# Two convolution layers: the product's halves interleaved, the second chunk's transform moved onto TensorE, the first chunk's sums opened with the stream

## The chip, the core and the metric

The kernel runs on one core of one Trainium2 chip. A core has five engines that run their own instruction streams and meet only at semaphores: TensorE (PE in the profile; its weight loads are PEld), VectorE (DVE), ScalarE (ACT), GpSimd (POOL) and SyncE (SP, which here only issues transfers). TensorE writes to PSUM; VectorE and ScalarE read PSUM and SBUF. Transfers (DMA) are issued by SP, ACT or POOL and carried out by 16 DMA engines that all issuers share.

The metric is the device time of one execution in microseconds (us); lower is better.

## The reference

A stream `x` of 2048 rows by 640 channels goes through four layers, each a normalisation, a layer function and a residual sum:

```python
x = A_u
x = x + _A_ref(_layernorm(x, axis=-1), ...)   # long convolution
x = x + _B_ref(_layernorm(x, axis=-1), ...)   # attention, 32 heads of 20, one shared key and value head
x = x + _A_ref(_layernorm(x, axis=-1), ...)
x = x + _B_ref(_layernorm(x, axis=-1), ...)
```

The convolution builds one kernel of length 2048 for each channel from 128 complex exponentials, and convolves each channel of the normalised stream with it:

```python
P = jnp.exp(logdA[:, :, None] * l[None, None, :])
K = jnp.einsum("dn,dnl,dn->dl", Cc, P, dB).real
Kf = rfft(pad(K)); Uf = rfft(pad(u transposed))
y = irfft(Uf * Kf)[:L] transposed + u * Dskip
```

So a convolution layer is, per channel: transform, complex product with the kernel's spectrum, inverse transform, residual sum.

## The kernel before

**Stages.** First the kernels `K` are generated (0 to about 300 us). Then follow convolution layer a with the kernels' spectra in front of it (to about 618 us), attention layer b (to about 1693 us), convolution layer c (to about 1940 us) and attention layer d. The change lies in `conv_layer`, which makes layers a and c; only a is called with `first=True`.

**Chunks.** A layer treats the 640 channels in five chunks of 128 (`NCH` = 5), numbered c = 0 to 4. Sequence position is split over 128 partitions and 16 columns `tau`, so the stream is `x[128, 16, 640]`. A chunk passes these steps:

1. `prepare(c)`: ScalarE writes the normalised chunk into `xn` (one buffer for all chunks, so chunk c+1's values wait for chunk c's matmuls), in 128x128 pieces (L761). TensorE multiplies with the transform weights `wf`, ScalarE copies the four sums (`z0` to `z3`) from PSUM into the chunk's spectrum `A`. There are two forms. `raw` (L574 matmuls, L576 copies) takes 16 normalised pieces and transforms each of the eight residues by itself; VectorE must then begin with `halve` (L587), one sum and one difference over 2048 columns each. `dense` (L608, L610) takes 24 pieces, eight of them the negatives of others, and streams pairs of them, so that the sums and differences come out of TensorE: twice the moving columns per matmul, and no `halve`. Chunks 0 and 1 use `raw`, the others `dense`.
2. Forward `fft8`: sixteen VectorE instructions between `A` and the scratch `B` (L114, L117).
3. The complex product with the kernel's spectrum `kh`. For chunks 0 to 3 this is `spread`: VectorE computes the four real products in place, in two halves of the rows h = 0 and 1, four instructions each (L845, L846, L847, L849), and the sums and differences are left to the DMA engines: POOL issues a transfer that adds `r` onto `ar` (L848) and one that adds `ki` onto `ai` (L850), 512 KB each, four in a chunk. Chunk 4 does the whole product on VectorE (L779).
4. Inverse `whole(A, +1)`: `halve` and `fft8` again, on the sums that the transfers have left in `A`.
5. `inverse(c, g)`, g = 0 to 3: TensorE multiplies with `wi` (L804) into one PSUM bank of 512 columns per g; two banks take turns. For chunk 3 alone (`NCH - 2`) the sum is opened with a matmul of the identity and the stream's own piece (L797).
6. `residual(c, g)`: VectorE adds the bank onto the stream (L815). For chunk 3, where the bank already holds the whole sum, ScalarE copies it (L813). `turn(g)` is one residual and, for g < 2, the next `inverse` of the same chunk.

**Order.** The layer runs under a manual schedule: each of PE, ACT and DVE executes in the order the program states, and stalls on the first instruction whose inputs are late. Around chunk c the program states: `spread(c)`; the load of the next `kh` on SP (it waits for `spread(c)`'s transfers, since there is one `kh` buffer, L711); the forward transform of chunk c+1 with the four turns of chunk c-1 woven in at places 2, 6, 10 and 14; `prepare(c+2)`; `whole(A)` of chunk c; `inverse(c, 0)` and `inverse(c, 1)`. So TensorE's order is: transform 0, transform 1, transform 2, inverse 0, transform 3, inverse 1, transform 4, inverse 2, inverse 3, inverse 4. During chunk 3 ScalarE also takes sums for the next normalisation, and the next attention layer's weights are made (layer a) or loaded (layer c, L926).

Of the kernel before, what the change touches and what calls it, by code (L numbers as in the profile page):

```python
# [16 lines left out]
ALU = mybir.AluOpType  # L17
# [9 lines left out]
NCH = D // DC  # L27
# [76 lines left out]
def fft8(nc, A, B, sg, low=None):  # L104

    ADD, SUB = ALU.add, ALU.subtract
    plus, minus = (ADD, SUB) if sg < 0 else (SUB, ADD)  # L110
    calls = []

    def tt(*a):
        calls.append(lambda: nc.vector.tensor_tensor(*a))  # L114

    def stt(*a):
        calls.append(lambda: nc.vector.scalar_tensor_tensor(*a, op0=ALU.mult, op1=ADD))  # L117

    low = A if low is None else low
    tt(B[:, 0:4], low[:, 0:4], low[:, 4:8], ADD)  # L120
    tt(B[:, 4:8], low[:, 0:4], low[:, 4:8], SUB)
    tt(B[:, 8:12:3], A[:, 8:10], A[:, 13:11:-1], plus)
    tt(B[:, 10:8:-1], A[:, 8:10], A[:, 13:11:-1], minus)
    tt(A[:, 0:2], B[:, 0:2], B[:, 2:4], ADD)
    tt(A[:, 8:10], B[:, 0:2], B[:, 2:4], SUB)
    tt(B[:, 0:2], A[:, 10:15:4], A[:, 11:16:4], ADD)
    if sg < 0:
        tt(B[:, 2:4], A[:, 11:16:4], A[:, 10:15:4], SUB)
    else:
        tt(B[:, 2:4], A[:, 10:15:4], A[:, 11:16:4], SUB)  # L130
    tt(A[:, 4:14:9], B[:, 4:6], B[:, 7:5:-1], plus)
    tt(A[:, 12:4:-7], B[:, 4:6], B[:, 7:5:-1], minus)
    if sg < 0:
        tt(B[:, 12:16:3], B[:, 0:3:2], B[:, 3:0:-2], ADD)
        tt(B[:, 14:12:-1], B[:, 0:3:2], B[:, 3:0:-2], SUB)
    else:
        tt(B[:, 12:16:3], B[:, 2::-2], B[:, 1:4:2], SUB)
        tt(B[:, 14:12:-1], B[:, 2::-2], B[:, 1:4:2], ADD)
    sp, sm = (RT_HALF, -RT_HALF) if sg < 0 else (-RT_HALF, RT_HALF)
    f0, f2, f1, f3s = B[:, 8:10], B[:, 10:12], B[:, 12:14], B[:, 15:13:-1]  # L140
    stt(A[:, 2:4], f1, RT_HALF, f0)
    stt(A[:, 10:12], f1, -RT_HALF, f0)
    stt(A[:, 6:16:9], f3s, sp, f2)
    stt(A[:, 14:6:-7], f3s, sm, f2)
    return calls


def weave(calls, between):

    for i in range(len(calls) + 1):  # L150
        for n, call in between:
            if n == i or (i == len(calls) and n > i):
                call()
        if i < len(calls):
            calls[i]()


class Net:
# [579 lines left out]
    def conv_layer(self, nm, first):  # L738
# [3 lines left out]
        tc, nc, cv = self.tc, self.nc, self.cvp  # L742
        B = self.B
        tt = nc.vector.tensor_tensor
        with tc.manual_schedule(engines={mybir.EngineType.PE, mybir.EngineType.Activation,
# [14 lines left out]
            def normal(out, c, tau, r, b):  # L760
                nc.scalar.activation(out, X(c, tau), AF.Identity, scale=r[:, tau : tau + 1],  # L761
                                     bias=b[:, tau : tau + 1])

            def normals(xn, c, t):

                for j in range(2):
                    i = 4 * j + t
                    normal(xn[:, i], c, 8 * j + t, rs, nmr)
                    normal(xn[:, 8 + 2 * i], c, 8 * j + t + 4, rs, nmr)
                    normal(xn[:, 9 + 2 * i], c, 8 * j + t + 4, rsm, nmrm)  # L770

            def new_xn(c):
                return cv.tile([P, 24, DC], F32, tag="xn", bufs=1, name=f"xn{nm}{c}")

            def m(a, c_):
                return a.rearrange("p (s c) d -> p s c d", c=2)[:, :, c_]
# [12 lines left out]
            def stream(c, g):  # L789
                return self.x[:, FIRST[g] : 16 : 4, c * DC : (c + 1) * DC]  # L790

            def inverse(c, g, A):
                y = self.ps1(f"y{nm}{c}{g}")
                v = A.rearrange("p s (k d) -> p s k d", k=2)
                whole = c == NCH - 2
                if whole:
                    nc.tensor.matmul(y, self.ident, stream(c, g), start=True, stop=False)  # L797
                for s in range(4):
                    tau = TAUS[4 * g + s]
                    t, j = tau % 8, tau // 8  # L800
                    i = 0
                    for kk in range(2):
                        for c_ in range(2):
                            nc.tensor.matmul(y[:, s * DC : (s + 1) * DC], self.wi[:, t, j, c_, kk],  # L804
                                             v[:, 2 * t + c_, kk], start=(i == 0 and not whole),
                                             stop=(i == 3 and (s == 3 or not whole)))
                            i += 1
                return y

            def residual(c, g, y):  # L810
                y = y.rearrange("p (t d) -> p t d", t=4)
                if c == NCH - 2:
                    nc.scalar.activation(stream(c, g), y, AF.Copy)  # L813
                else:
                    tt(stream(c, g), y, stream(c, g), ALU.add)  # L815
                if c == NCH - 1:
                    self.stats_last(g)


            def prepare(c):  # L820

                xn = new_xn(c)
                for t in range(4):
                    if c < 2:
                        for tau in (t + 4, t + 12, t, t + 8):
                            normal(xn[:, tau], c, tau, rs, nmr)
                    else:
                        normals(xn, c, t)
                return (self.raw if c < 2 else self.dense)(xn, f"{nm}{c}", (c + 1) % 3)

            As = {0: prepare(0)}
            khs = {0: self.load_spectrum(0)}
            self.wi = cv.tile([P, 8, 2, 2, 2, P], F32, tag="wi", name="wi")
# [4 lines left out]
            def spread(A, kh):  # L838


                add = nc.gpsimd.dma_start
                for h in range(2):
                    s = slice(4 * h, 4 * h + 4)
                    ar, ai, kr, ki, r = m(A, 0)[:, s], m(A, 1)[:, s], m(kh, 0)[:, s], m(kh, 1)[:, s], R[:, s]
                    nc.vector.scalar_tensor_tensor(r, ai, -1.0, ki, op0=ALU.mult, op1=ALU.mult)  # L845
                    tt(ki, ar, ki, ALU.mult)  # L846
                    tt(ar, ar, kr, ALU.mult)  # L847
                    add(ar, r, accum_op=ALU.add)  # L848
                    tt(ai, ai, kr, ALU.mult)  # L849
                    add(ai, ki, accum_op=ALU.add)  # L850

            turn = None
            for c in range(NCH):
                A = As.pop(c)
                if c == NCH - 1:
                    late = [(1, lambda turn=turn: turn(0)), (2, lambda turn=turn: turn(1)),
                            (4, lambda turn=turn: turn(2)), (5, lambda turn=turn: turn(3))]
                    late = sorted(late + [(3 + k, a[0]) for k, a in enumerate(pieces)]
                                  + [(5 + k, a[1]) for k, a in enumerate(pieces)], key=lambda a: a[0])
                    weave(product(A, khs.pop(c)) + fft8(nc, A, B, +1), late)  # L860
                else:
                    spread(A, khs.pop(c))
                    khs[c + 1] = self.load_spectrum(c + 1)
                    woven = [] if turn is None else [
                        (n, lambda turn=turn, g=g: turn(g)) for g, n in enumerate((2, 6, 10, 14))]
                    N = As[c + 1]
                    weave(self.whole(N, -1) if c == 0 else fft8(nc, N, B, -1), woven)
                    if c + 2 < NCH:
                        As[c + 2] = prepare(c + 2)
                    if c + 2 == NCH - 1:  # L870
                        self.wfs.pop().close()
                    if c == NCH - 2:
                        scr = new_xn("s").rearrange("p a d -> p (a d)")

                        def dump(n):
                            return scr[:, 1280 + NA * (n % 4) : 1280 + NA * (n % 4) + NA]

                        self.stats_setup(nm)
                        for g in range(4):
                            self.stats_first(g, dump)  # L880
                        pieces = self.attn_weights(scr, nm == "a")
                    weave(self.whole(A, +1), ())
                ys = [inverse(c, g, A) for g in range(2)]

                def turn(g, c=c, A=A, ys=ys):

                    residual(c, g, ys[g])
                    if g < 2:
                        ys.append(inverse(c, g + 2, A))
# [489 lines left out]
```

## Time and profile before

| what | value |
|---|---|
| three runs | 3024.99, 3022.26, 3023.30 us |
| median | 3023.3 us |
| the profiled execution | 3024.13 us |
| its span, first to last instruction | 3022.3 us |
| TensorE, VectorE, ScalarE busy in the span | 92%, 46%, 80% |
| mean granted TensorE clock | 0.951 |

A line of the timeline reads: start, duration, engine, source line, operation, destination and sources, shapes, count of merged instructions, and in brackets how long the engine had been idle before and which instruction ended that wait. `Aa`, `za`, `ya`, `xna` are the spectrum, the forward sums, the inverse sums and the normalised chunk of layer a; `Ac`, `zc`, `yc`, `xnc` those of layer c. An fp32 matmul shows as two records, so an `inverse` of 16 matmuls is 32 records, and a chunk's inverse 128. A row of the view by stretches reads: stretch, its length, then busy time and count for PE, PEld, DVE, ACT and POOL, the granted TensorE clock, the mean busy share of the 16 DMA engines, and GB/s. "DMA to landing" is the time from the start of the issue to the last byte.

### The profile page before, as it was taken

Reading aid. Unit: us, or ns where it says so; the run is one execution under the profiler, and the core shown is the slowest. Engines: PE = TensorE matmul, PEld = TensorE weight load, DVE = VectorE, ACT = ScalarE, POOL = GpSimd, SP = SyncE. Lnnn points to the kernel's source line nnn. Section 1 sums busy time; section 2 is a strip of 40 time slices with the busy share of each in tenths; the row PEclk is TensorE's granted clock in tenths of the full one; section 3 lists DMA queues with packets and bytes.
Section 4 is the critical chain, followed back from the end, with each engine's and each line's share of the span. In section 5 each row is a group of like instructions: output and inputs, shape, how many; then the busy total and the mean of one; then the engine's idle time right before and its main releaser. Section 6 shows DMA issues by size and latency. Waiting matters only on the chain. (4 is left out here: it accounts for less than half of the span.)

```text
span 3022.3 us, 52462 instructions
## 1 busy us (share of the span) xinstructions
PE 2769.4 (92%) x21696; PEld 1266.8 (42%) x21696; DVE 1384.6 (46%) x1784; ACT 2421.5 (80%) x2894; POOL 86.3 (3%) x149
## 2 busy tenths in 40 slices
PE   2676978898999999999999888798999999999999
PEld 0333978775233323333233678673233233333233
DVE  7999899942122232322323499721222223222223
ACT  5888351444999999999999524238999999999997
POOL 0001001000000000000000011000000000000000
PEclk9656999999999999999999989899999999999999
DMA  6114555433200010100000256131100100110100
GB/s 145 33 22 112 175 154 112 97 116 115 81 22 25 22 27 21 27 24 23 25 22 20 86 112 145 39 130 56 28 24 23 43 22 25 39 28 21 43 19 23
DMA packets 126000, 175.60 MB, mean 58 GB/s; under 512 B 59460, under 2 KB 81988, under 8 KB 122132
## 3 DMA queue, kind: packets, MB, share of 16 engines
q1 hardware_dynamic: 102680, 137.70, 15.7%
q0 software_dynamic: 21104, 33.45, 5.5%
q8 instruction: 175, 2.87, 0.4%
q10 hardware_dynamic: 1968, 0.98, 0.1%
q14 instruction: 73, 0.60, 0.1%
HBM read 95.22 MB, written 48.04 MB: 47 GB/s over the span
## 5 line engine op out<-in xcount | busy, mean ns | idle before, releaser
L1177 ACT ACTIVATE pt<-scd 128x1024 f32<-128x1024 f32 x1024 | 942.2, 1116 | 6.9 <-PE scd L1173 5.5
L1177 ACT ACTIVATE pt<-scb 128x1024 f32<-128x1024 f32 x1024 | 942.1, 1116 | 6.5 <-PE scb L1173 5.1
L1187 PE MATMUL pod<-pt,vt 128*32 128x512 f32 x4096 | 546.9, 606 | 4.4 <-DVE on L1204 0.2
L1187 PE MATMUL pob<-pt,vt 128*32 128x512 f32 x4096 | 546.4, 605 | 4.4
L1173 PE MATMUL scb<-qpb,kt 62*128 62x512 f32 x2048 | 385.8, 451 | 5.9 <-DVEq L1122 5.6
L1173 PE MATMUL scd<-qpd,kt 62*128 62x512 f32 x2048 | 385.7, 451 | 5.9 <-PEq L1122 5.5
L1173 PEld LDWEIGHTS scd<-qpd,kt 62*128 62x128 f32 x2048 | 166.1, 185 | 402.2 <-ACT pt L1177 392.4
L1173 PEld LDWEIGHTS scb<-qpb,kt 62*128 62x128 f32 x2048 | 166.1, 185 | 401.6 <-ACT pt L1177 391.9
L1235 DVE TENSOR_TENSOR x<-pyd,x 128x320 f32<-128x320 f32 x146 | 71.8, 492 | 560.7 <-PE pyd L1247 560.7
L1235 DVE TENSOR_TENSOR x<-pyb,x 128x320 f32<-128x320 f32 x146 | 71.8, 492 | 547.5 <-PE pyb L1247 547.5
L1207 DVE RECIPROCAL rc<-rc 128x512 f32<-128x512 f32 x62 | 207.9, 3353 | 2.1
L1187 PEld LDWEIGHTS pod<-pt,vt 128*32 128x32 f32 x4096 | 80.6, 108 | 177.4 <-issue 159.5
L1187 PEld LDWEIGHTS pob<-pt,vt 128*32 128x32 f32 x4096 | 80.6, 108 | 177.5 <-issue 159.5
L804 PE MATMUL yc<-Ac,wi 128*128 128x128 f32 x640 | 80.2, 291 | 32.1 <-DVE Ac L114 20.4
L804 PE MATMUL ya<-Aa,wi 128*128 128x128 f32 x640 | 79.8, 290 | 32.2 <-DVE Aa L114 22.8
L1247 PE MATMUL pyb<-wo,ot 128*32 128x320 f32 x1168 | 105.3, 432 | 0.0
L1247 PE MATMUL pyd<-wo,ot 128*32 128x320 f32 x1168 | 105.3, 432 | 0.0
L804 PEld LDWEIGHTS yc<-Ac,wi 128*128 128x128 f32 x640 | 79.7, 207 | 34.9 <-DVE x L815 11.8
L804 PEld LDWEIGHTS ya<-Aa,wi 128*128 128x128 f32 x640 | 79.1, 206 | 35.1 <-DVE Aa L114 24.0
L610 ACT ACTIVATE Aa<-za 128x1024 f32<-128x1024 f32 x12 | 12.3, 1025 | 101.6 <-PE za L608 101.6
L608 PE MATMUL zc<-xnc,wf 128*128 128x256 f32 x384 | 85.3, 384 | 2.4 <-ACT xnc L761 2.3
L608 PE MATMUL za<-xna,wf 128*128 128x256 f32 x384 | 83.7, 380 | 2.7 <-ACT xna L761 2.7
(323 smaller groups left out, 3110.3 us busy)
## 6 DMA issues: line engine op xcount, KB each, us to landing
Akh<-kh SPq DMA_DIRECT2D x10, 2048.0 KB
kh<-Ak SPq DMA_DIRECT2D x5, 2048.0 KB
qhd<-qh SPq DMA_DIRECT2D x40, 256.0 KB
qld<-ql SPq DMA_DIRECT2D x40, 256.0 KB
qpb<-qhd SPq DMA_DIRECT2D x256, 40.0 KB
qpd<-qhd SPq DMA_DIRECT2D x256, 40.0 KB
ot<-on SPq DMA_DIRECT2D x216, 40.0 KB
wf<-in_c_wf POOLq DMA_DIRECT2D x16, 512.0 KB, 8.0
```

The costliest lines, as they stand in the source:

```text
L608: nc.tensor.matmul(zv[:, :, c, kk], self.wf[:, t + 4 * h, j, c, kk], x, start=(n == 0), stop=(n == 3))
L610: nc.scalar.activation(A.rearrange("p (o s) d -> p o s d", o=2)[:, :, 2 * t : 2 * t + 2], z.rearrange("p (c o e) -> p o c e", c=2, o=2), A ...
L804: nc.tensor.matmul(y[:, s * DC : (s + 1) * DC], self.wi[:, t, j, c_, kk], v[:, 2 * t + c_, kk], start=(i == 0 and not whole), stop=(i == 3 ...
L1173: nc.tensor.matmul(sc[:, 512 * par : 512 * par + 512], kt[rows, 128 * t : 128 * t + 128], qps[nb, hg, pr][rows], start=True, stop=True)
L1177: nc.scalar.activation(pt, sc, AF.Exp, scale=SCALE)
L1187: nc.tensor.matmul(po[32 * j : 32 * j + 32], vt[:, t], pts[step, j // 2][:, 512 * (j % 2) : 512 * (j % 2) + 512], start=(t == 0), stop=(t ...
L1207: nc.vector.reciprocal(rc, rc)
L1235: nc.vector.tensor_tensor(xh, py, xh, ALU.add)
L1247: nc.tensor.matmul(py[j : j + m], o[:, 128 * i + j : 128 * i + j + m], w[:, 320 * half : 320 * half + 320], start=start, stop=stop)
```

## The change

Three edits, all in `conv_layer`:

- The residual of chunk 0 is treated like that of chunk 3: the sum in PSUM is opened with identity times stream, and ScalarE copies it back instead of VectorE adding. Both layers.
- `halved` is the number of chunks that use `raw`. It is 2 in layer c, as before, and 1 in layer a: there chunk 1 uses `dense`, and its forward transform is `fft8` without `halve`.
- `spread` issues its four steps for both halves in turn (step 1 for h = 0 and 1, step 2 for both, and so on), where it did all four for h = 0 and then for h = 1. The transfers stay behind the instruction that makes their target. Chunks 0 to 3 of both layers.

```diff
@@ inverse / residual
-                whole = c == NCH - 2
+                whole = c in (0, NCH - 2)
...
-                if c == NCH - 2:
+                if c in (0, NCH - 2):
                     nc.scalar.activation(stream(c, g), y, AF.Copy)
                 else:
                     tt(stream(c, g), y, stream(c, g), ALU.add)
@@ prepare
+            halved = 1 if first else 2
+
...
-                    if c < 2:
+                    if c < halved:
                         for tau in (t + 4, t + 12, t, t + 8):
                             normal(xn[:, tau], c, tau, rs, nmr)
                     else:
                         normals(xn, c, t)
-                return (self.raw if c < 2 else self.dense)(xn, f"{nm}{c}", (c + 1) % 3)
+                return (self.raw if c < halved else self.dense)(xn, f"{nm}{c}", (c + 1) % 3)
@@ spread
+                ops = [[], [], [], []]
                 for h in range(2):
...
-                    nc.vector.scalar_tensor_tensor(r, ai, -1.0, ki, op0=ALU.mult, op1=ALU.mult)
-                    tt(ki, ar, ki, ALU.mult)
-                    tt(ar, ar, kr, ALU.mult)
-                    add(ar, r, accum_op=ALU.add)
-                    tt(ai, ai, kr, ALU.mult)
-                    add(ai, ki, accum_op=ALU.add)
+
+                    def fourth(ai=ai, kr=kr, ki=ki):
+                        tt(ai, ai, kr, ALU.mult)
+                        add(ai, ki, accum_op=ALU.add)
+
+                    def third(ar=ar, kr=kr, r=r):
+                        tt(ar, ar, kr, ALU.mult)
+                        add(ar, r, accum_op=ALU.add)
+
+                    ops[0].append(lambda r=r, ai=ai, ki=ki: nc.vector.scalar_tensor_tensor(
+                        r, ai, -1.0, ki, op0=ALU.mult, op1=ALU.mult))
+                    ops[1].append(lambda ar=ar, ki=ki: tt(ki, ar, ki, ALU.mult))
+                    ops[2].append(third)
+                    ops[3].append(fourth)
+                for a in ops:
+                    for call in a:
+                        call()
@@ the loop over chunks
-                    weave(self.whole(N, -1) if c == 0 else fft8(nc, N, B, -1), woven)
+                    weave(self.whole(N, -1) if c + 1 < halved else fft8(nc, N, B, -1), woven)
```

## Prediction, made before the changed kernel was run

> **What bounds the kernel now.** I read the view by stretches first, since the span's shares mix stages: the two attention layers fill most of it and the change does not touch them, so they can only move in time.
>
> ```profile
> span 3022.3 us, 52462 instructions
> ```
>
> ```profile
> 389.30:476.30 87.00, 61.57 (x385) 57.10 (x386) 85.79 (x107) 32.67 (x73) 10.31 (x8) 0.86 0.55 124
> 476.30:560.30 84.00, 84.00 (x515) 77.39 (x514) 77.24 (x92) 27.23 (x67) 10.61 (x9) 1.00 0.54 111
> 1795.60:1880.00 84.40, 84.40 (x516) 77.40 (x514) 77.62 (x93) 27.61 (x69) 10.26 (x8) 1.00 0.53 116
> ```
>
> From chunk 1's transform to the end of chunk 0's inverse (389 to 476 us in layer a) VectorE works 85.8 of 87 us and TensorE 61.6. From there to the last forward transform TensorE works all 84 us at full clock and VectorE waits. Layer c has the same second half. So VectorE sets when TensorE's unbroken run begins, and TensorE sets its length: work taken off VectorE pays only if TensorE can start its run earlier. The timeline of TensorE (layer a, then c) shows where it waits:
>
> ```profile
> 407.95 27.46 PE L608 MATMUL za<-xna,wf 128*128 128x256 f32 x126 [0.46 <-ACT xna L761]
> 448.24 9.95 PE L804 MATMUL ya<-Aa,wi 128*128 128x128 f32 x64 [12.83 <-DVE Aa L114]
> 467.56 8.87 PE L804 MATMUL ya<-Aa,wi 128*128 128x128 f32 x64 [9.37 <-DVE x L815]
> 476.27 27.79 PE L608 MATMUL za<-xna,wf 128*128 128x256 f32 x128
> 577.32 1.02 PE L797 MATMUL ya<-x,ident 128*128 128x512 f32 x2
> 581.75 1.02 PE L797 MATMUL ya<-x,ident 128*128 128x512 f32 x2
> ```
>
> ```profile
> 1766.42 7.31 PE L804 MATMUL yc<-Ac,wi 128*128 128x128 f32 x64
> 1785.38 10.36 PE L804 MATMUL yc<-Ac,wi 128*128 128x128 f32 x64 [11.66 <-DVE x L815]
> 1795.58 27.79 PE L608 MATMUL zc<-xnc,wf 128*128 128x256 f32 x128
> ```
>
> Waits of 12.83, 9.37 and 11.66 us stand in chunk 0's inverse. Two of them end with a residual (L815): TensorE needs the PSUM bank back and VectorE reaches the addition only after the next product. The waits cost twice: 64 records that take 7.31 us without a break take 9.95 and 10.36 after one (the mean clock of that stretch is 0.86).
>
> **Edit 1, chunk 0's residual on ScalarE (both layers).** Removed: four VectorE additions at 0.60 each (466.82 to 467.42 below) and the wait for them. Added: an identity matmul per g. The period from one opened sum to the next is 581.75 - 577.32 = 4.43 us, so an opened inverse takes 17.7. Moved: four copies enter ScalarE's queue ahead of the 24 pieces of chunk 3, which before were written long in advance.
>
> ```profile
> 389.28 6.26 ACT L761 ACTIVATE xna<-x,nmra,rsa 128x128 f32<-128x128 f32 x16
> 405.49 0.87 ACT L761 ACTIVATE xna<-x,nmra,rsa 128x128 f32<-128x128 f32 x2
> 436.37 0.87 ACT L761 ACTIVATE xna<-x,nmra,rsa 128x128 f32<-128x128 f32 x2
> 581.95 0.60 ACT L813 ACTIVATE x<-ya 128x512 f32<-128x512 f32 x1 [3.83 <-PE ya L804]
> ```
>
> The last copy can start 0.20 us after the sums (581.95 against 581.75), takes 0.60, overlaps its successor by 0.1, and only then come chunk 3's pieces: 0.7. From the first piece to the end of a dense transform is 407.95 + 27.46 - 405.49 = 29.92 us. Chunk 3's transform thus ends 30.6 us after chunk 0's inverse, where 27.79 would do: 2.8 us of new wait, in each layer, not hidden by anything.
>
> **Edit 2, chunk 1 dense in layer a.** VectorE loses `halve`, 428.18 - 423.65 = 4.53 us. TensorE gains twice the columns. Its pieces start at 389.28 as before; the transform ends at 389.28 + 29.92 = 419.20. Chunk 2's pieces follow 0.96 later (436.37 against 435.41), and its transform ends at 420.16 + 29.92 = 450.08, 14.7 later than now. The cover is the 12.83 and 9.37 us of waiting.
>
> **Edit 3, the product's order.** The VectorE rows:
>
> ```profile
> 414.06 1.23 DVE L845 SCALAR_TENSOR_TENSOR Ra<-Aa,Akh 128x1024 f32<-128x1024 f32 x1
> 415.32 1.23 DVE L846 TENSOR_TENSOR Akh<-Aa,Akh 128x1024 f32<-128x1024 f32 x1
> 416.58 1.22 DVE L847 TENSOR_TENSOR Aa<-Aa,Akh 128x1024 f32<-128x1024 f32 x1
> 417.72 1.22 DVE L849 TENSOR_TENSOR Aa<-Aa,Akh 128x1024 f32<-128x1024 f32 x1
> ...
> 423.65 2.29 DVE L587 TENSOR_TENSOR B<-Aa 128x2048 f32<-128x2048 f32 x1
> ...
> 428.18 2.35 DVE L114 TENSOR_TENSOR B<-B 128x1024 f32<-128x1024 f32 x2
> ...
> 439.37 2.29 DVE L587 TENSOR_TENSOR B<-Aa 128x2048 f32<-128x2048 f32 x1
> ...
> 454.97 1.22 DVE L845 SCALAR_TENSOR_TENSOR Ra<-Aa,Akh 128x1024 f32<-128x1024 f32 x1
> ...
> 466.82 0.69 DVE L815 TENSOR_TENSOR x<-ya,x 128x512 f32<-128x512 f32 x1
> 467.42 1.28 DVE L114 TENSOR_TENSOR B<-Aa 128x512 f32<-128x512 f32 x2
> ...
> 1772.80 1.22 DVE L845 SCALAR_TENSOR_TENSOR Rc<-Ac,Akh 128x1024 f32<-128x1024 f32 x1
> ...
> 1824.47 2.36 DVE L114 TENSOR_TENSOR B<-Ac 128x1024 f32<-128x1024 f32 x2 [1.49 <-ACT Ac L610]
> ...
> 1866.39 2.36 DVE L114 TENSOR_TENSOR B<-Ac 128x1024 f32<-128x1024 f32 x2 [1.49 <-ACT Ac L610]
> ...
> 1881.55 2.29 DVE L587 TENSOR_TENSOR B<-Ac 128x2048 f32<-128x2048 f32 x1
> ```
>
> L845 and L846 are followed 1.26 us after their start by an instruction that overwrites what they read; L847 by an independent one after 1.14. Interleaved, all eight are spaced 1.14: 9.1 instead of 9.6 us, 0.47 saved per product. [...]
>
> The other side is the transfers. The first add now stands behind the fifth product instead of the third.
>
> ```profile
> 418.39 1.33 POOL L848 DMA_DIRECT2D Aa<-Ra  x1 [94.01 <-DVE Aa L847]
> ...
> 424.03 1.41 POOL L850 DMA_DIRECT2D Aa<-Akh  x1
> ...
> 1859.50 1.29 POOL L848 DMA_DIRECT2D Ac<-Rc  x1 [34.80 <-ACT Ac L610]
> ...
> 1865.37 1.26 POOL L850 DMA_DIRECT2D Ac<-Akh  x1
> ```
>
> ```profile
> DMA to landing us min/median/max: 8.6/9.2/9.8
> ```
>
> ```profile
> 420.50:432.50 12.00, 12.00 (x58) 10.55 (x57) 11.90 (x11) 2.05 (x2) 3.07 (x3) 1.00 1.18 167
> ```
>
> ```profile
> DMA to landing us min/median/max: 15.2/15.2/15.2
> ```
>
> ```profile
> 1865.33 0.32 SPq L926 DMA_DIRECT2D wh<-whd  x1
> ```
>
> The fourth add of chunk 0 lands at 424.03 + 9.8 = 433.8, 15.4 after the first issue, and meanwhile the DMA engines are busy throughout (share 1.18): the four drain one behind the other, so the last lands 15.4 after the first is issued, however close the other three follow. The first is issued 1.81 after L847 starts (418.39 - 416.58); L847 now starts 4 x 1.14 = 4.6 after the product's start, so the issue comes at 6.4 and the last landing at 21.8, where it was 19.8. The inverse transform waits for it, and behind it VectorE's whole queue; so does the next `kh` load on SP, 2 us later but with more than 10 us to spare. In chunk 3 of layer c the load L926 (SP, issued when the last transform ends) shares the engines: there the last lands 1865.37 + 15.2 - 1859.50 = 21.1 after the first issue. The load now comes earlier relative to the adds, but the same bytes drain, so I keep 21.1.
>
> [...]
>
> **The sum, layer a.** Forward 11.19 us is 428.18 to 439.37, inverse transform 15.6 is 439.37 to 454.97. VectorE: product 414.06 to 423.2; forward of chunk 1 to 434.4; last landing 435.9, so inverse transform 435.9 to 451.5. Chunk 0's first sums could start 8.9 after its start (448.24 - 439.37), at 444.8; TensorE comes at 450.08 and is the later one. Its inverse ends at 467.8, chunk 3's transform at 498.4, now 476.27 + 27.79 = 504.06: **5.6 us earlier**. VectorE then stands ready at 498.0 (inverse of chunk 1 from 473.3, landing-bound, to 488.9, product to 498.0) and needs the transform's last copy at 499.5, so TensorE stays the bound and the rest of the layer follows shifted.
>
> **The sum, layer c.** Only edits 1 and 3 act. Chunk 0's inverse runs 1766.42 to 1784.1, chunk 3's transform ends at 1814.8, now 1823.37: 8.6 earlier, ready for VectorE at 1815.9. VectorE: chunk 1's product starts at 1772.3, landing 1794.1 (the forward transform is done at 1792.6: 1.5 us of waiting), inverse to 1809.7, product to 1818.9. Now VectorE is later by 3 us. With 11.2 + 4 x 0.60 = 13.6 for the forward of chunk 3 and its turns: 1832.5 (landing 1831.5), inverse to 1848.1, product to 1857.2. The bank it returns at 1821.9 lets the last transform end 8.3 earlier than now, so VectorE's next forward starts at 1858.1 instead of 1866.39. Its inverse would start 15.16 later (1866.39 to 1881.55), at 1873.2, but the adds, first issued at 1848.1 + 6.4 = 1854.5, land 21.1 later: 1875.6. Against 1881.55 that is **5.9 us earlier**, and VectorE is busy from there to the end of the layer.
>
> Together 11.6 us. The sum is made against the profiled execution, 3024.13 us (span 3022.3 and 1.8 around it), giving 3012.5; the median of the runs is 0.8 lower, so I forecast 3011.7.
>
> **The rivals.**
> - *The adds do not bind.* If a landing counted from the last issue, no VectorE wait would arise; layer c gains 8.6, the total is 14.2, the time 3009.1. Against it: the share of 1.18 during all four. Chance 0.12.
> - *Layer a gains nothing.* Its 5.6 is a small difference: 22.2 us of waits and 4.4 of slow clock removed, against 14.7 of dense transform, 3.3 of identity matmuls and 2.8 of new wait. If the clock lagged or the pieces came later, it is eaten: 3023.3 - 5.9 = 3017.4. Against it: in 389 to 435 us the records already run at the full rate of the unbroken run (27.46 for 126). Chance 0.14.
> - *Slower: four adds in a bunch drain worse.* Now they come in pairs 4.5 us apart. They take about 3.1 us each once flowing; at 4.2 the later landings in chunks 1 to 3 eat both layers' gains, and at 4.5 each they cost 4 us in layer a and 4.8 in c: 3032. For it: chunk 3's landing of 15.2 us shows what competition does. Against it: the third and fourth already queue behind others at the same rate. Chance 0.08.
>
> **The numbers.** My case has 0.62, with its own range 3009.5 to 3015; 0.04 is left for what I have not seen. The range over the first three cases, widened a little, is 3008 to 3018. A change of 0.2% (6 us) is about what a measurement of this kernel can tell from none. My case, the first rival and half of the second lie beyond it: faster 0.83; same 0.09; slower 0.08.
>
> **What would show it.** In layer a a dense transform of chunk 1 ending near 419 and no wait of 9 us or more on TensorE until 550; chunk 0's inverse in one piece of about 17.7; some 2 us of waiting on xn before chunk 3's transform in both layers; product instructions spaced 1.14; in layer c a wait of about 1.5 us on VectorE at the inverse transform of chunk 1 and about 2.4 at chunk 3. The forecast is wrong if chunk 0's inverse still waits for VectorE, if the landings come more than 24 us after a product's start, or if the attention layers change length.

## The result, and the profile after

The changed kernel takes 3016.49 us (median of 12 runs, 3014.54 to 3019.28) against 3024.01 for the kernel before (12 runs): 7.5 us less, ratio 0.9975, 95% interval 0.9968 to 0.9983. The profiled execution took 3015.11 us. Its page and its view by stretches:

```profile
span 3013.3 us, 52501 instructions
```

```profile
389.30:476.30 87.00, 79.47 (x408) 68.46 (x409) 81.80 (x106) 35.21 (x76) 10.36 (x8) 0.98 0.54 121
472.11:556.11 84.00, 83.54 (x507) 76.58 (x507) 74.98 (x91) 34.30 (x86) 10.66 (x9) 1.00 0.56 113
1784.00:1868.00 84.00, 83.55 (x495) 76.24 (x495) 78.40 (x97) 32.72 (x81) 10.34 (x8) 0.98 0.59 126
```

In the first stretch TensorE now works 79.5 of 87 us, where it worked 61.6. Its timeline, the forward transforms of layer a, chunk 0's inverse between them, and two transforms of layer c:

```profile
391.37 0.70 PE L608 MATMUL za<-xna,wf 128*128 128x256 f32 x2 [2.26 <-ACT xna L761]
392.53 29.15 PE L608 MATMUL za<-xna,wf 128*128 128x256 f32 x126 [0.46 <-ACT xna L761]
...
425.09 27.46 PE L608 MATMUL za<-xna,wf 128*128 128x256 f32 x126 [0.46 <-ACT xna L761]
452.39 1.02 PE L797 MATMUL ya<-x,ident 128*128 128x512 f32 x2
...
465.68 1.02 PE L797 MATMUL ya<-x,ident 128*128 128x512 f32 x2
...
472.11 0.70 PE L608 MATMUL za<-xna,wf 128*128 128x256 f32 x2 [1.84 <-ACT xna L761]
473.27 27.46 PE L608 MATMUL za<-xna,wf 128*128 128x256 f32 x126 [0.46 <-ACT xna L761]
...
1734.14 29.81 PE L608 MATMUL zc<-xnc,wf 128*128 128x256 f32 x128 [2.26 <-ACT xnc L761]
...
1784.66 29.15 PE L608 MATMUL zc<-xnc,wf 128*128 128x256 f32 x126 [0.46 <-ACT xnc L761]
```

The long waits in chunk 0's inverse are gone; its sums follow each other every 4.43 us. But the 126 records of chunk 1's transform take 29.15 us and those of chunk 2's 27.46: the same instructions. The clock (the third number from the end) in the 6 us in which the slow one begins:

```profile
392.00:394.00 2.00, 1.54 (x5) 1.26 (x5) 1.97 (x4) 2.00 (x7) 0.00 (x0) 0.72 0.72 279
394.00:396.00 2.00, 2.00 (x6) 1.56 (x5) 2.00 (x4) 2.00 (x7) 0.00 (x0) 0.50 1.01 434
396.00:398.00 2.00, 2.00 (x10) 1.70 (x10) 1.97 (x4) 2.00 (x6) 0.00 (x0) 0.92 0.50 213
```

After a wait of 2.26 us TensorE was granted 0.50 of its clock from 394 to 396 us, and 0.72 and 0.92 in the 2 us on either side. VectorE's and POOL's rows show the new order of the product and the waits for the adds:

```profile
415.34 2.36 DVE L857 SCALAR_TENSOR_TENSOR Ra<-Aa,Akh 128x1024 f32<-128x1024 f32 x2
...
424.43 3.56 DVE L114 TENSOR_TENSOR B<-Aa 128x1024 f32<-128x1024 f32 x4
...
437.23 2.29 DVE L587 TENSOR_TENSOR B<-Aa 128x2048 f32<-128x2048 f32 x1 [1.77 <-DMA Aa<-Akh]
...
475.68 2.29 DVE L587 TENSOR_TENSOR B<-Aa 128x2048 f32<-128x2048 f32 x1 [2.72 <-issue]
...
1791.74 2.29 DVE L587 TENSOR_TENSOR B<-Ac 128x2048 f32<-128x2048 f32 x1 [1.92 <-DMA Ac<-Akh]
...
1873.65 2.29 DVE L587 TENSOR_TENSOR B<-Ac 128x2048 f32<-128x2048 f32 x1 [1.70 <-DMA Ac<-Akh]
```

```profile
421.69 2.63 POOL L855 DMA_DIRECT2D Aa<-Ra  x2 [95.91 <-DVE Aa L854]
...
1852.59 2.59 POOL L855 DMA_DIRECT2D Ac<-Rc  x2 [33.20 <-issue]
```

The experiments are compared by the length of the two layers, since the code outside them is the same. Layer a is counted from chunk 0's first matmul to attention b's first normalised piece, layer c from its own first normalised piece to that of attention d. A row at the edge of a view counts only the instructions inside the view. Before, then after:

```profile
373.60 2.66 PE L574 MATMUL za<-xna,wf 128*128 128x128 f32 x20 [1.49 <-ACT xna L761]
616.94 0.92 ACT L1018 ACTIVATE x<-x,nmrna,rsna 128x640 f32<-128x640 f32 x1 [5.21 <-PE ya L804]
1700.85 1.26 ACT L761 ACTIVATE xnc<-x,nmrc,rsc 128x128 f32<-128x128 f32 x3 [1.42 <-DVE rsmc L750]
1932.99 0.92 ACT L1018 ACTIVATE x<-x,nmrnc,rsnc 128x640 f32<-128x640 f32 x1 [1.48 <-DVE nmrnc L682]
```

```profile
374.39 1.32 PE L574 MATMUL za<-xna,wf 128*128 128x128 f32 x8 [1.49 <-ACT xna L761]
613.92 0.92 ACT L1032 ACTIVATE x<-x,nmrna,rsna 128x640 f32<-128x640 f32 x1 [5.20 <-PE ya L804]
1698.32 3.96 ACT L761 ACTIVATE xnc<-x,nmrc,rsc 128x128 f32<-128x128 f32 x10 [1.42 <-DVE rsmc L750]
1924.33 0.92 ACT L1032 ACTIVATE x<-x,nmrnc,rsnc 128x640 f32<-128x640 f32 x1 [1.48 <-DVE nmrnc L682]
```

Layer a goes from 243.34 to 239.53 us (-3.8), layer c from 232.14 to 226.01 (-6.1). The attention layers keep their lengths within 0.5 us.

All runs stand in one table. The runs e and f were made on one chip and the runs g on another, where the kernel before takes 3026.14 us, so kernels are compared by the difference to the kernel before on the same chip. The ratio is the record's own estimate and can differ from the quotient of the two medians by up to 0.0004. The layers are those of one profiled execution each. Layer a's length holds a part that no edit touches: VectorE comes to chunk 0's product 96.14 to 96.22 us after a wait for the generated kernels (before 414.06 - 317.86 = 96.20, the change 415.34 - 319.12 = 96.22), in all thirteen traces, but that wait ends anywhere from 316.5 to 320.3 us, while the count begins with TensorE's first matmul. So the distance from that matmul to the product is 40.5 us before, 41.0 in the change and 41.9 in f1, but 37.8 in e1, 38.0 in e2 and 38.6 in f2: layer a of these three can look up to 2.7 us shorter than their edits make it.

| kernel | median us | difference | ratio (95%) | layer a | layer c |
|---|---|---|---|---|---|
| before | 3024.01 | | | 243.34 | 232.14 |
| the change | 3016.49 | -7.5 | 0.9975 (0.9968 to 0.9983) | 239.53 | 226.01 |
| e1: edit 1 alone | 3013.36 | -10.9 | 0.9966 (0.9953 to 0.9978) | 233.51 | 225.33 |
| e2: edit 2 alone | 3018.36 | -5.9 | 0.9982 (0.9973 to 0.9992) | 235.45 | 231.95 |
| e3: edit 3 alone | 3024.87 | +0.7 | 1.0003 (0.9993 to 1.0012) | 242.91 | 231.47 |
| e12: edits 1 and 2 | 3016.25 | -8.0 | 0.9972 (0.9962 to 0.9983) | 239.76 | 225.36 |
| f1: the change, waits filled | 3014.02 | -9.8 | 0.9967 (0.9955 to 0.9980) | 236.90 | 225.76 |
| f0: the change, adds earlier | 3016.14 | -7.7 | 0.9975 (0.9966 to 0.9984) | 237.74 | 224.89 |
| f2: the change, two sums opened | 3011.81 | -12.0 | 0.9961 (0.9947 to 0.9976) | 233.44 | 226.01 |
| f4: two sums in chunks 0 to 2 | 3008.70 | -15.1 | 0.9949 (0.9935 to 0.9963) | 235.72 | 222.49 |
| g1: f4, waits filled | 3009.37 | -16.8 | 0.9949 (0.9935 to 0.9962) | 236.34 | 222.04 |
| g2: edit 1, waits filled | 3009.37 | -16.8 | 0.9947 (0.9933 to 0.9960) | 236.50 | 222.94 |
| g3: edits 1 and 2, waits filled | 3011.25 | -14.9 | 0.9952 (0.9938 to 0.9965) | 236.94 | 222.46 |

f4, g1, g2 and g3 are clear of the change by their intervals (g3 by a hair: 0.9965 against 0.9968), and e3 on the other side; the rest can't be told from the change by their times. Where those are told apart below, it is by rows.

### The profile page after: what moved, and what is told of

It is laid out like the page before. It is cut to its first block, busy times and chain, and to the rows that moved or that the text cites. A ratio compares the mean times of both kernels' runs of the same rounds, so it can differ in the third digit from the quotient of the medians.

```text
span 3013.3 us, 52501 instructions
## 1 busy us (share of the span) xinstructions
PE 2787.7 (93%) x21712; PEld 1275.9 (42%) x21712; DVE 1371.8 (46%) x1774; ACT 2429.1 (81%) x2910; POOL 86.6 (3%) x149
## 5 line engine op out<-in xcount | busy, mean ns | idle before, releaser
L608 PE MATMUL za<-xna,wf 128*128 128x256 f32 x512 | 114.0, 384 | 7.7 <-ACT xna L761 7.7
L608 PEld LDWEIGHTS za<-xna,wf 128*128 128x128 f32 x512 | 97.9, 192 | 23.1 <-ACT xna L761 9.7
```

Source lines behind the costliest of these rows:

```text
L608: nc.tensor.matmul(zv[:, :, c, kk], self.wf[:, t + 4 * h, j, c, kk], x, start=(n == 0), stop=(n == 3))
```

## The experiments

### One edit at a time

Edit 1 alone is the change with `raw` for chunk 1 and the product in its old order:

```diff
-                whole = c == NCH - 2
+                whole = c in (0, NCH - 2)
...
-                if c == NCH - 2:
+                if c in (0, NCH - 2):
```

> Edit 1 alone: chunk 0's sums opened with the stream and copied by ScalarE in both layers; chunk 1 stays raw in layer a, the product keeps the old order. My theory (the adds drain from the first issue on, TensorE's waits in chunk 0's inverse are what the change removes): layer a 4.3 us earlier (VectorE, with halve still in its queue, becomes the bound at chunk 3's forward transform), layer c 8.1 us earlier, because the first add keeps its early place and the inverse transform of chunk 3 finds the sums landed; together 12 us faster than before, that is as fast as the full change or faster, less up to 2 us where TensorE's clock falls to half behind the new wait. Rival (each edit brings a share of its own, the residual mainly frees 4 x 0.6 us of VectorE per layer): 3 to 5 us faster than before and slower than the full change.

Measured: 10.9 us faster than before, where 12 less up to 2 was expected. TensorE's timeline of e1 in layer a:

```profile
409.47 29.15 PE L608 MATMUL za<-xna,wf 128*128 128x256 f32 x126 [0.46 <-ACT xna L761]
447.07 5.63 PE L804 MATMUL ya<-Aa,wi 128*128 128x128 f32 x32 [7.59 <-DVE Aa L114]
...
467.83 0.70 PE L608 MATMUL za<-xna,wf 128*128 128x256 f32 x2 [1.83 <-ACT xna L761]
```

There is still a wait of 7.59 us for VectorE in front of chunk 0's inverse, and the first sum after it is slow (5.63 us for 32 records). But the inverse begins at 447.07, which is 5.3 us earlier than in the change, where TensorE is held by the longer transforms until 452.39. (Counted from chunk 0's first matmul it is 6.05: 447.07 - 375.12 against 452.39 - 374.39.) So what the opened sums gain doesn't need edit 2.

Edit 2 alone:

```diff
+            halved = 1 if first else 2
...
-                    if c < 2:
+                    if c < halved:
...
-                return (self.raw if c < 2 else self.dense)(xn, f"{nm}{c}", (c + 1) % 3)
+                return (self.raw if c < halved else self.dense)(xn, f"{nm}{c}", (c + 1) % 3)
...
-                    weave(self.whole(N, -1) if c == 0 else fft8(nc, N, B, -1), woven)
+                    weave(self.whole(N, -1) if c + 1 < halved else fft8(nc, N, B, -1), woven)
```

> Edit 2 alone: chunk 1 of layer a transformed whole by TensorE, residual of chunk 0 on VectorE, product in the old order. My theory: VectorE loses 4.5 us at chunk 0, TensorE starts chunk 0's inverse warm at about 450 us and then waits some 6 us for the bank that VectorE gives back; layer a about 4 us earlier, layer c unchanged: 4 us faster. Rival (the extra transform is not hidden): TensorE's added 14.7 us outweigh the wait removed, no gain or slower.

Measured: 5.9 us faster, where 4 was expected; layer c is unchanged (231.95 against 232.14). Layer a is 7.9 us shorter from the first matmul, but 5.4 from chunk 0's product on. TensorE's timeline of e2 (the last row is cut by the end of the view):

```profile
452.38 7.31 PE L804 MATMUL ya<-Aa,wi 128*128 128x128 f32 x64
462.00 7.41 PE L804 MATMUL ya<-Aa,wi 128*128 128x128 f32 x64 [2.32 <-DVE x L815]
469.25 2.97 PE L608 MATMUL za<-xna,wf 128*128 128x256 f32 x13
```

The 14.7 us of longer transform fill the wait before the inverse; of the two waits of 12.83 and 9.37 us one of 2.32 is left. So edits 1 and 2 spend the same idle time, and their gains (10.9 and 5.9) don't add up: both together, below, give 8.0.

Edit 3 alone:

```diff
-                    tt(ar, ar, kr, ALU.mult)
-                    add(ar, r, accum_op=ALU.add)
-                    tt(ai, ai, kr, ALU.mult)
-                    add(ai, ki, accum_op=ALU.add)
...
+                    ops[2].append(third)
+                    ops[3].append(fourth)
+                for a in ops:
+                    for call in a:
+                        call()
```

> Edit 3 alone: the product's halves interleaved, nothing else. My theory: the product takes 9.1 instead of 9.6 us, the last add lands 21.8 instead of 19.8 us after the product's start; only the two products ahead of TensorE's unbroken run count (about 0.9 us per layer), and in layer c chunk 3's inverse transform then waits about 1.2 us for its adds, which takes the gain back there: within 1 us of before. Rival (spacing is what counts): 8 x 0.47 = 3.8 us faster.

Measured: no difference (+0.7 us, interval on both sides of 1). The products take 9.09 us as in the change, and VectorE waits for the adds only in chunk 3 of layer c (1.01 us). TensorE's waits in chunk 0's inverse are still there (12.06 and 8.58 us in layer a, 10.68 in layer c). That they hide the order is a reading; this run doesn't show it.

### The change without edit 3

Edits 1 and 2 with the product in its old order.

> The change without edit 3: opened sums and dense chunk 1, the product in the old order. My theory: layer a as in the full change, layer c 2.2 us better than it, because at chunk 3 the last add lands before VectorE asks: about 2 us faster than the full change, no wait on the adds at any inverse transform but at most 0.5 us. Rival (interleaving helps by its 0.47 per product): 2 to 4 us slower than the full change.

Measured: 3016.25, the same as the change; the 2 us expected did not come. VectorE has no wait for adds left in layer c, as expected (in layer a one of 0.99 us stays in front of chunk 1's inverse transform), but the transforms of chunk 3 start slow in both layers: 126 records in 29.15 us. This raised a second theory: a short wait in front of a dense transform costs TensorE its clock, and behind that limit the adds are hidden. In the nine traces without filling, 31 transforms start with such a wait (1.83 to 2.26 us, then two records, then up to 0.46). In layer c all 13 were slow, in layer a 7 of 18: 28.71 to 29.15 us for 126 records where the others take 27.46, or 29.74 to 29.84 for all 128.

### Filling the waits

Two matmuls of the identity with 512 columns go ahead of the first real matmul of the dense transforms of chunks 1 to 3. They write into the bank that the transform is about to open anew, so their results are overwritten. The call passes `fill` for these chunks:

```diff
-    def dense(self, xn, nm, k):
+    def dense(self, xn, nm, k, fill=False):
...
+            if fill and t == 0:
+                for _ in range(2):
+                    nc.tensor.matmul(z[:, 0:512].rearrange("p (c k d) -> p c k d", c=2, k=2), self.ident,
+                                     self.wf[:, 0, 0], start=True, stop=True)
...
+                return self.dense(xn, f"{nm}{c}", (c + 1) % 3, c < NCH - 1)
```

> The full change with two identity matmuls of 512 columns (on the weights, into a bank that the transform then overwrites; no result changes) put into the wait ahead of each dense transform of chunks 1 to 3. My theory now (the waits of 1.8 to 2.3 us before the dense transforms drop TensorE to half clock, which makes a transform 29.15 instead of 27.46 us; the change has five such transforms where before has two): every dense transform takes 27.5 after the filled wait, the granted clock stays 1.00 there, and the time falls by 2 to 4 us below the full change, with less spread between runs. Rival (the missing 4 us of the forecast lie elsewhere, in the start of the layer or in the attention layers): the same time as the full change within 1 us, or slower, since TensorE has more to do.

Measured: 3014.02 us, 9.8 under the kernel before against 7.5 of the change: 2.3 less, as expected, though not clear of the noise. The runs spread over 1.0 us where the change's spread over 4.7. TensorE's timeline of f1, and its clock in the stretch in which the change had 0.50:

```profile
389.08 1.88 PE L604 MATMUL za<-wf,ident 128*128 128x512 f32 x4
391.51 0.70 PE L612 MATMUL za<-xna,wf 128*128 128x256 f32 x2 [0.54 <-ACT xna L765]
392.66 27.46 PE L612 MATMUL za<-xna,wf 128*128 128x256 f32 x126 [0.46 <-ACT xna L765]
...
1782.88 27.46 PE L612 MATMUL zc<-xnc,wf 128*128 128x256 f32 x126 [0.45 <-ACT xnc L765]
```

```profile
394.00:396.00 2.00, 2.00 (x11) 1.75 (x10) 2.00 (x4) 2.00 (x7) 0.00 (x0) 1.00 0.97 418
```

All five transforms take 27.46 us, and so do all 16 of the four kernels with filling. The transform starts no earlier, since the pieces of xn come as before; only the clock differs. That the unfilled short wait is what costs the clock is thus shown (slow in 20 of 31 without the filling, in none of 16 with it). Layer a is 2.6 us shorter, of which 1.7 stand at chunk 3's transform and 0.9 appear only at the layer's end; layer c is only 0.25 shorter, although two transforms there are faster.

### The order of the product

Why layer c kept its length was asked twice. First without filling, by an order that issues the adds earlier (first sum's add behind the third product, as before the change):

```diff
-                for a in ops:
-                    for call in a:
-                        call()
+                for k in ((0, 0), (1, 0), (2, 0), (0, 1), (3, 0), (1, 1), (3, 1), (2, 1)):
+                    ops[k]()
```

> The full change with the product's eight steps in another order: the first half's first add again behind the third step, the rest spaced so that only two steps follow one they depend on. My theory: the product takes 9.3 us, the last add lands 19.8 us after its start, VectorE waits for no add at chunks 0 and 1; layer c gains up to 0.7 us, layer a nothing since TensorE bounds it: 0 to 1.5 us faster than the full change. Rival (the adds' delay is what keeps the change from its forecast): 3 us or more faster.

Measured: 3016.14, the same as the change. In layer c VectorE no longer waits for the adds, and the layer is 1.1 us shorter, with its transforms of chunks 2 and 3 still slow (29.74 us for 128 records, 29.15 for 126). The profiled execution of f0 isn't typical of its runs: it took 3011.99, 4.2 under their median, at a mean granted clock of 0.982 where the other profiles have 0.951 to 0.959. Then with filling: the change without edit 3 and with the fill of f1.

> Edits 1 and 2 with the product in its old order, and the same fill. With the clock held, the difference to the filled full change is the product's order alone. Theory of the prediction: the adds are spread over the product and land before VectorE asks in layer c, so 2 us under the filled full change, about 3012. Rival, that TensorE sets the end of chunk 3 in both layers, so that VectorE's order is free: within 1 us of 3014.

Measured: 3011.25 us, 14.9 under the kernel before against 9.8 of f1: 5.1 less where 2 was expected, with intervals that overlap. Of this 3.3 is seen in layer c (222.46 against 225.76) and nothing in layer a; the rest isn't placed. VectorE in chunk 3 of layer c, f1 and then g3:

```profile
1868.82 1.28 DVE L117 SCALAR_TENSOR_TENSOR Ac<-B 128x512 f32<-128x512 f32 x2
1872.30 2.29 DVE L587 TENSOR_TENSOR B<-Ac 128x2048 f32<-128x2048 f32 x1 [2.19 <-DMA Ac<-Akh]
```

```profile
1868.88 1.28 DVE L117 SCALAR_TENSOR_TENSOR Ac<-B 128x512 f32<-128x512 f32 x2
1870.20 2.29 DVE L587 TENSOR_TENSOR B<-Ac 128x2048 f32<-128x2048 f32 x1
```

VectorE comes to this point 0.7 us later in f1, counted from the layer's start (1697.63 and 1698.37), and there waits 2.19 us for the adds, where g3 doesn't wait; the last 0.5 us of the 3.3 come after it. So layer c had two limits side by side, the clock and the adds. Taking away one alone left 225 to 226 us (e12 225.36, f1 225.76), both 222.5: the reason why e12 showed nothing. Edit 1 alone, in the old order too, shows the same step with the filling: 225.33 in e1, 222.94 in g2.

### Does edit 2 help beside edit 1?

Edit 1 alone with the fill, in front of chunks 2 and 3.

> Edit 1 alone (chunk 1 dense by the residual) with the same fill before the dense transforms of chunks 2 and 3. Theory that the opened sums of edit 2 keep inverse 0 busy for longer than the wait that they remove: 3010.5 to 3011, 3 us under the filled full change (3014.0), with chunk 3's transform of layer a ending 3 us earlier from the same start. Rival, that edit 1 alone was only lucky in its clock: equal to the filled full change within 1 us.

What the expectation calls the opened sums of edit 2 must be edit 2's longer transforms: the opened sums are edit 1's and stand in both kernels. Measured: 3009.37 us, 16.8 under the kernel before and so 7.0 under f1, more than expected, but for another reason. Layer a is 236.50 against 236.90 of f1 and 236.94 of g3; the lead over f1 lies in layer c (222.94 against 225.76), where edit 2 does nothing and only the order of the product differs. TensorE in layer a, g2 and then g3:

```profile
448.61 5.91 PE L808 MATMUL ya<-Aa,wi 128*128 128x128 f32 x32 [11.85 <-DVE Aa L114]
...
469.64 0.70 PE L612 MATMUL za<-xna,wf 128*128 128x256 f32 x2
```

```profile
451.69 1.02 PE L801 MATMUL ya<-x,ident 128*128 128x512 f32 x2
...
471.41 0.70 PE L612 MATMUL za<-xna,wf 128*128 128x256 f32 x2
```

From chunk 0's first matmul (374.10 and 375.38) to chunk 3's transform it is 95.5 us with a wait of 11.85 in it and 96.0 without any: edit 2 turns a wait for VectorE into work for TensorE and gains nothing. My theory that it costs 3 us fell. The remaining lead of e1 in layer a (233.51) isn't edit 2 either: in its profile the product of chunk 0 came 37.8 us after the first matmul, in g2 40.3, by code that is the same in both. Counted from that product, the rest of the layer takes 195.7 us in e1 and 196.2 in g2.

### Fewer opened sums

In the change all four sums of chunk 0 are opened and copied by ScalarE. Here only the first two:

```diff
-                whole = c in (0, NCH - 2)
+                whole = c == NCH - 2 or (c == 0 and g < 2)
...
-                if c in (0, NCH - 2):
+                if c == NCH - 2 or (c == 0 and g < 2):
```

> The full change with only the first two of chunk 0's four sums opened with the stream and copied by ScalarE; the other two are added by VectorE as before. My theory: chunk 3's pieces are written during the last two sums, so the 1.8 us wait before its transform goes, and 2 x 0.82 us of identity matmuls with it: chunk 3's transform ends 3.5 to 5.5 us earlier in both layers. Layer a gains 3.5 to 5 us; layer c less, 0 to 2 us, because VectorE is the later one there. 4 to 6 us faster than the full change. Rival (VectorE is the bound and the 4 x 0.6 us matter): slower than the full change by 1 to 2 us.

Measured: 3011.81 us, 12.0 under the kernel before and so 4.5 under the change, as expected, though the intervals overlap. TensorE's timeline of f2:

```profile
457.94 10.88 PE L804 MATMUL ya<-Aa,wi 128*128 128x128 f32 x96
468.65 27.79 PE L608 MATMUL za<-xna,wf 128*128 128x256 f32 x128
```

Two identity sums less (0.86 each) and no copies behind the inverse: the third and fourth sum run on, and chunk 3's pieces are long written when TensorE asks, so the transform starts without a wait and takes 27.79 us, as the same 128 records do at a granted clock of 1.00 in the kernel before (476.30 to 560.30). It starts 93.66 us after chunk 0's first matmul instead of 97.72. Only the first two banks have to come back during the inverse. The whole gain lies in layer a (6.1 us from the first matmul, 3.7 from chunk 0's product on); layer c is 226.01 in both.

Then the same for chunks 1 and 2 as well, with `raw` for chunk 1 again and f0's order:

```diff
-                whole = c in (0, NCH - 2)
+                whole = c == NCH - 2 or (c < NCH - 2 and g < 2)
...
-                if c in (0, NCH - 2):
+                if c == NCH - 2 or (c < NCH - 2 and g < 2):
...
-            halved = 1 if first else 2
+            halved = 2
```

> A version from the findings: chunk 1 raw again in layer a, the product in the early-add order, and for chunks 0, 1 and 2 the first two sums opened with the stream and copied by ScalarE, the other two added by VectorE. My theory: TensorE never waits for VectorE to return a bank and never for ScalarE before chunk 3; layer a 8 to 11 us earlier than before, layer c 7 to 9 us: 15 to 19 us faster than before, 3005 to 3009 us. Rival (what edit 1 alone reached is the floor, the rest is bound by VectorE and the adds): about 3012 us.

Measured: 3008.70 us, 15.1 under the kernel before and so 7.6 under the change, at the low end of the 15 to 19 expected. With the fill before chunk 2's transform:

> f4 with two identity matmuls of 512 columns put into the wait before the dense transform of chunk 2, in both layers (their results are overwritten). Half-clock theory: the dense transforms of chunk 2 take 27.5 us each instead of up to 29.2, so 2 to 2.5 us under f4, about 8 to 9 per thousand under... the kernel before, near 3006 us, and the runs spread under 2 us. Rival, that the remaining waits of f4 do not lose the clock or that VectorE binds there: the same as f4 within 0.7 us.

Measured: 3009.37 on the other chip, 16.8 under the kernel before against 15.1 of f4: 1.7 less, between the rival's 0.7 and the 2 to 2.5 expected, and with the same interval as f4, so the time decides for neither. The rows speak for the rival: both transforms of chunk 2 take 27.46 instead of 28.87 and 28.79, but the layers keep their length (236.34 and 222.04 against 235.72 and 222.49), and in layer a TensorE only waits longer for VectorE behind the transform (11.70 us against 10.51). The runs spread over 4.4 us, not under 2 as expected. f4, g1, g2 and g3 can't be told apart.

## Why the prediction was right, and where its sum was off

The sign and the main mechanism held, and the time, 3016.5, lies inside the range; but of 11.6 us only 7.5 came (9.0 between the two profiled executions), and the time falls outside the likeliest case's own 3009.5 to 3015, towards the second rival's 3017.4.

- **Layer c held.** 5.9 us forecast, 6.1 measured. The adds set the end as forecast: VectorE waits 1.70 us for them in chunk 3 (2.4 forecast), the last lands 21.06 us after the first issue (1873.65 - 1852.59, 21.1 forecast); in chunk 1 it waits 1.92 (1.5 forecast). At the place where the forecast counts, the start of chunk 3's inverse transform, the gain is 5.4 (1881.55 - 1700.85 against 1873.65 - 1698.32); the other 0.8 came behind it, and the forecast had nothing for it, so that 5.9 and 6.1 are so close is in part luck. The slow clock that chunk 3's transform had here too (0.50 from 1786 to 1788 us, 29.15 us for 126 records) was not what VectorE waited for: the transform ended at 1813.81, and VectorE was through with its product of chunk 2 only at 1816.42.
- **Edit 3's terms held.** The product takes 424.43 - 415.34 = 9.09 us (9.1 forecast), where it took 423.65 - 414.06 = 9.59 before. The first add is issued 6.35 after the product's start (6.4) and the last lands 21.9 after it (21.8). What I did not draw from these terms is that the edit's balance is a loss: the wait it makes, 2.19 us with the clock held, takes its place in front of everything that VectorE still has to do, and layer c is 3.3 us longer than without the edit (f1 against g3, one profiled execution each); layer a is the same. The 0.47 us per product count for nothing where the inverse transform waits for the landing.
- **Edit 1's terms held.** The period of 4.43 us, the wait before chunk 3's transform (1.84 on xn), no wait of 9 us or more until 550. That opening all four sums was needless (f2) was in those numbers and not drawn: the 2.8 us of new wait belonged to the third and fourth sum.
- **The step that failed is edit 2's, in layer a:** "the transform ends at 389.28 + 29.92 = 419.20". The row behind 29.92 is of a transform that kept its clock after its wait (1.00 from 406.79 to 435.41 us). In the change it took 1.69 us more (29.15 against 27.46). From there all later steps are late by that and by a start 0.8 us later in code that isn't changed (374.39 against 373.60): chunk 3's transform ends at 473.27 + 27.46 = 500.73, forecast 498.4, before 504.06. So 3.3 us instead of 5.6. With the wait filled, 27.46 came back and layer a was 2.6 us shorter (f1), 1.7 of them by the end of chunk 3's transform.
- **The second rival had the mechanism.** "If the clock lagged" was written there and set aside by the one transform in layer a that kept its clock. (Its slow clock of 4.4 us is 4.2 by the rows: 9.95 - 7.31 and 8.87 - 7.31. With 4.2 its terms do give 5.6.) The trace of before held the other answer in layer c, in the same transform's row there:

```profile
1736.74 29.84 PE L608 MATMUL zc<-xnc,wf 128*128 128x256 f32 x128 [2.26 <-ACT xnc L761]
```

  In layer a the same 128 records end 28.62 us after their start (407.95 + 27.46 - 406.79); 29.84 is 1.2 more, after the same wait, with a granted clock of 0.50 from 1738 to 1740 us. The change has five such transforms where the kernel before had two.
- **The other rivals fell.** The adds do bind: three waits on VectorE end with a landing, and a fourth, of 2.72 us in layer a's chunk 1, for which the trace names no releaser, ends 16.55 us after its first add was issued (475.68 - 459.13). They drain little worse in a bunch: 15.5 us from the first issue to the last landing in chunk 0 (437.23 - 421.69) and in chunk 1 of layer c, 16.55 in chunk 1 of layer a, where 15.4 was forecast; the third rival needed 4.2 us for each of the four.
- **The last 1.5 us** between the profiled pair (9.0) and the medians (7.5) are open: the changed kernel's runs spread over 4.7 us, and the profiled one is 1.4 under their median.

## What to carry to other kernels

Price a transform behind a short wait with the clock it may lose (up to 1.69 us here), and look at every row of its kind in the trace, not at the one that suits the sum; two dummy matmuls in the wait kept the transform at 27.46 us in all 16 cases here, though their gain in time alone wasn't clear of the noise. Before two edits are added up, ask whether they spend the same idle time. Compare layers from a point that no edit touches, on the engine that is late. Where two limits stand side by side, take both away before an edit is called worthless. Opening chunk 0's sums with the residual did away with the waits of 9.37 and 11.66 us for VectorE to return a PSUM bank (e1): do it for the banks that must come back, not for all.

## What the hardware showed that was not expected

- Waits of 1.83 to 2.26 us in front of TensorE, with two records and up to 0.46 us more behind them, were followed by a slow transform in 20 of 31 cases, always in layer c (13 of 13) and only at times in layer a (7 of 18). Each cost up to 1.69 us (29.15 against 27.46 for 126 records). Where the clock was read, it was 0.50 from 394 to 396 and from 1786 to 1788 us in the change, back at 1.00 from 398 and 1790, and 0.50 from 1738 to 1740 in the kernel before, back at 1.00 from 1742. Why layer c always loses and layer a not is open.
- The first 32 records of chunk 0's inverse after a wait of 7.6 to 11.9 us take 5.6 to 6.2 us instead of 3.73 (e1, f4, g1, g2), so a long wait there carries 1.8 to 2.5 us with it. In the kernel before, behind the wait of 12.83 us, the granted clock was 0.50 from 448 to 452 us, 0.60 to 454 and 1.00 from there on.
- The distance from chunk 0's first matmul to its product, in code that no kernel here changed on VectorE, was 37.8 to 41.9 us over the traces, as large as some of the differences that were to be explained. It is settled ahead of the layer: the product follows the end of VectorE's wait for the generated kernels by 96.14 to 96.22 us in every trace, and that wait ends anywhere from 316.5 to 320.3. What moves its end is open.
